# Attention inside a fused MLP kernel: phi's column maximum as one strided reduction on VectorE, and the scaling of the identity by it on GpSimd

## The chip, the core and the metric

One core of a Trainium2 chip runs the whole program. Its engines are TensorE (PE in the profile; its weight loads are PEld), VectorE (DVE), ScalarE (ACT), GpSimd (POOL) and SyncE (SP), which here only issues DMAs. Each engine takes its own instructions strictly in order and waits on semaphores for the others. The metric is the time of one execution on the device in microseconds, lower being better. The kernel before took 1745.2 us (median of 3 runs, 1739.94 to 1746.93).

## What is computed

```python
def _attn_ref(q, k, v, phi):                       # 8 batches, 8 heads, 576 rows, 64 wide; phi has 32 columns
    a = phi - np.max(phi, axis=2, keepdims=True)   # maximum over the 576 rows, per column
    a = np.exp(a)
    a = a / (np.sum(a, axis=2, keepdims=True) + 1e-09)
    k_m = np.einsum('bhsm,bhsd->bhmd', a, k)
    v_m = np.einsum('bhsm,bhsd->bhmd', a, v)
    scores = scale * np.matmul(q, k_m.transpose(0, 1, 3, 2))
    ...
    return np.matmul(attn, v_m)

# then, on the 4608 x 512 result:
h = x @ w_in;  x = (h - np.tanh(h)) @ w_out                              # layer 1, 2048 wide
h = x @ w_in;  out = np.where(h > 0, h, np.exp(np.minimum(h, 0)) - 1) @ w_out   # layer 2
```

The weights of the layers come as 64-bit floats and are converted on the chip.

## The kernel before

Attention is done in 16 units, each one batch and four of its heads. A unit's phi lies in SBUF as a tile `ph` of 96 partitions x 4 heads x 6 chunks x 32 columns: row s of phi is partition s // 6, chunk s % 6. Its column maximum is made in these steps (`Attention.unit`, lines 115 to 141):

- Lines 119 to 121, VectorE: the maximum over the six chunks in three elementwise operations: chunks 0 to 2 with 3 to 5 into `top` (384 elements per partition), then two of 128 elements into `cmax`. `top` takes a buffer of tag `pT`, of which there is one; the transposed weights `pT` of the unit before live in it until GpSimd's `phl` has read them.
- Line 127, TensorE: transposes `cmax` (96 x 128) into `mT`, a PSUM tile.
- Line 129, VectorE: `nmax`, the maximum of each row of `mT`: one number for each of the 128 pairs of head and column.
- Line 131, VectorE: `dmax`, the identity matrix with row i scaled by `nmax[i]`.
- Line 134, TensorE: `bmax` = ones x `dmax`, which spreads the 128 maxima over 96 partitions. Line 138, ScalarE: copies it to `bm`.
- Line 140: `a = ph - bm`, on VectorE in units 0 and 1, and on GpSimd from unit 2 on (`eng`). Line 146, ScalarE: exp.

After that TensorE contracts `a` with k and v into `km` (lines 155 and 158), VectorE divides by the sums (`rs`, `kk`, `vbd`, lines 164 to 170), and the scores (`sc`, `s`, `smax`, `pT`, `phl`) follow.

A unit is a Python generator. Each `yield` ends its part of a round, and one round of all live units is written out at a time, so the order of instructions on each engine is the order in which the program writes them; there is no scheduler behind it. From unit 2 on (`spaced`) some steps have an extra `yield`. The main loop goes over the blocks of layer 1 and has two rounds for each half of a block: one between the first and the second group of `x_ps` matmuls, one behind the second. In every half it writes: the matmuls `h_ps` of layer 1 (line 357), their activation on ScalarE (`t`, `u`, `s`, lines 368 to 370) and GpSimd (`v`, line 375), matmuls `x_ps` of the block four steps back (line 405), a round of the units and of the weights' conversion, the split of the previous activation `g` (ScalarE line 392, GpSimd line 393), more `x_ps`, then on VectorE the end of the activation (`h_ps`, `s`, `s`, lines 384 to 386), then again a round. The conversion of a piece of weights runs over ScalarE (`cv_m`, line 48), VectorE (`cv_m` and `cv_a`, lines 50 to 55), ScalarE (line 58) and GpSimd (`w`, line 60). `vw_ps` (lines 327 and 344) multiplies converted weights into the attention's value tiles. Units start at fixed rounds (0, 1, 7, 13, 23, 29, 35 and so on up to 99). PSUM tiles of the units, `x_ps` and `vw_ps` share three buffers. From about 440 us on attention is over; the rest of layer 1 and layer 2 (from about 900 us) follow.

Of the kernel before, what the change touches and what calls it, by code (L numbers as in the profile page):

```python
# [8 lines left out]
F32 = mybir.dt.float32  # L9
# [4 lines left out]
ALU = mybir.AluOpType  # L14
AX = mybir.AxisListType
# [3 lines left out]
B, H, S, D, M = 8, 8, 576, 64, 32  # L19
# [43 lines left out]
class Attention:  # L63
# [43 lines left out]
    def unit(self, u, nxt, eng, first_p=None):  # L107

        nc, wk, sm = self.nc, self.wk, self.sm
        b, g = divmod(u, 2)  # L110
        ident = self.ident
# [3 lines left out]
        ph = self.loaded.pop((u, "phi"))  # L115
        row = lambda name: wk.tile([128, 4, M], F32, tag="cmax", name=name)
        cmax = row("cmax")[:96]
        top = wk.tile([128, S], F32, tag="pT", name="top")[:96, :12 * M].rearrange("p (h c m) -> p h c m", h=4, c=3)
        nc.vector.tensor_tensor(top, ph[:, :, 0:3], ph[:, :, 3:6], op=ALU.max)
        nc.vector.tensor_tensor(cmax, top[:, :, 0], top[:, :, 1], op=ALU.max)  # L120
        nc.vector.tensor_tensor(cmax, cmax, top[:, :, 2], op=ALU.max)
        yield
        spaced = u >= 2
        if spaced:
            yield
        mT = ps_tile([128, 96], "mT")
        nc.tensor.transpose(mT, cmax.rearrange("p h m -> p (h m)"), ident[:96, :96])
        nmax = sm.tile([128, 1], F32, tag="nmax", name="nmax")
        nc.vector.tensor_reduce(nmax, mT, axis=AX.X, op=ALU.max)
        dmax = row("dmax").rearrange("p h m -> p (h m)")  # L130
        nc.vector.tensor_scalar(dmax, ident, nmax, None, op0=ALU.mult)
        yield
        bmax = ps_tile([96, 4, M], "bmax")
        nc.tensor.matmul(bmax, lhsT=self.ones[:, :96], rhs=dmax, start=True, stop=True)
        if spaced:
# [5 lines left out]
                          op=ALU.subtract)  # L141
# [74 lines left out]
        pT = wk.tile([128, S], F32, tag="pT", name="pT")  # L216
# [303 lines left out]
def moe_kernel(tc, q, k, v, phi, w1, w2, w3, w4, out):  # L520
    nc = tc.nc
    with ExitStack() as top, tc.manual_schedule():
# [105 lines left out]
        for u in range(2 * B):  # L628
            units.at((0, 1, 7, 13, 23, 29, 35, 41, 47, 53, 59, 65, 78, 85, 92, 99)[u], unit(u))
# [264 lines left out]
```

## Time and profile before

| | |
|---|---|
| median of 3 runs | 1745.2 us |
| the profiled execution | 1745.33 us, of it 1743.5 us span |
| TensorE busy | 1636.6 us (94%) |
| VectorE busy | 1220.5 us (70%) |
| ScalarE busy | 943.2 us (54%) |
| GpSimd busy | 766.4 us (44%) |
| TensorE's mean granted clock | 0.97 of full speed |

The profile is of one execution. Its timeline gives each instruction's start and duration, the idle time of its engine just before it, and what ended that idle time (an arrow to engine, tile and line). The waits sum such idle times by the waiting and the awaited instruction. The groups sum instructions of one line and shape. The table by stretches gives the busy time of each engine in a stretch of the span, so that the stages can be told apart. A busy TensorE is one that has matmuls under way; at half of its clock the same matmuls take up to twice as long.

### The profile page before, as it was taken

Reading aid. Unit: us, or ns where it says so; the run is one execution under the profiler, and the core shown is the slowest. Engines: PE = TensorE matmul, PEld = TensorE weight load, DVE = VectorE, ACT = ScalarE, POOL = GpSimd, SP = SyncE. Lnnn points to the kernel's source line nnn. Section 1 sums busy time; section 2 is a strip of 40 time slices with the busy share of each in tenths; the row PEclk is TensorE's granted clock in tenths of the full one; section 3 lists DMA queues with packets and bytes.
Section 4 is the critical chain, followed back from the end, with each engine's and each line's share of the span. In section 5 each row is a group of like instructions: output and inputs, shape, how many; then the busy total and the mean of one; then the engine's idle time right before and its main releaser. Section 6 shows DMA issues by size and latency. Waiting matters only on the chain.

```text
span 1743.5 us, 30389 instructions
## 1 busy us (share of the span) xinstructions
PE 1636.6 (94%) x11632; PEld 1513.9 (87%) x11632; DVE 1220.5 (70%) x1804; ACT 943.2 (54%) x1697; POOL 766.4 (44%) x545
## 2 busy tenths in 40 slices
PE   5659899898998999999989999999999999999998
PEld 4548888787898999999989999999999999999997
DVE  5778776678899999998965555555555555555554
ACT  2446756677878888898853333333333333333332
POOL 3246555545666676676752222222222222222222
PEclk9669999999998999999999999999999999999999
DMA  8755664567566456666588311211112112211110
GB/s 212 203 152 155 187 181 156 173 191 232 192 218 200 161 189 216 218 218 213 185 246 320 119 61 51 60 61 61 50 60 62 61 61 61 61 55 55 55 32 24
DMA packets 145000, 238.42 MB, mean 137 GB/s; under 512 B 12504, under 2 KB 106712, under 8 KB 142808
## 3 DMA queue, kind: packets, MB, share of 16 engines
q1 hardware_dynamic: 144856, 236.49, 42.7%
q8 instruction: 92, 1.51, 0.4%
q14 instruction: 52, 0.43, 0.1%
HBM read 159.78 MB, written 75.50 MB: 135 GB/s over the span
## 4 chain that ended last, share of the span: by engine, by line
PE 74%; DVE 9%; DMA 6%; ACT 6%; issue 3%; POOL 2%; SPq 0%; DVEq 0%; ACTq 0%; POOLq 0%
PE h_ps L461 24%; PE o_ps L498 23%; PE x_ps L405 15%; PE h_ps L357 8%; DMA p<-p_dram 2%; PE vw_ps L327 2%; DMA phi<-in_phi_dram 1%; ACT t L368 1%; PE vw_ps L344 1%; DVE s L386 1%; DVE s L385 1%; DMA kv<-in_v_dram 1%; DMA xr<-x_dram 1%; DMA w_dram<-wst 1%; ACT u L369 1%
## 5 line engine op out<-in xcount | busy, mean ns | idle before, releaser
L405 PE MATMUL x_ps<-g,w 128*128 128x288 f32 x3072 | 442.3, 298 | 9.1 <-DVE s L203 4.7
L487 POOL TENSOR_TENSOR e<-hm,e 128x512 fp32r<-128x512 f32 x144 | 186.5, 1295 | 587.1 <-ACT e L486 429.7
L461 PEld LDWEIGHTS h_ps<-x,wi 128*128 128x128 f32 x3456 | 429.7, 190 | 11.9 <-issue 0.2
L461 PE MATMUL h_ps<-x,wi 128*128 128x256 f32 x3456 | 433.3, 281 | 0.0
L405 PEld LDWEIGHTS x_ps<-g,w 128*128 128x128 f32 x3072 | 420.7, 190 | 13.5 <-DVE s L203 5.2
L498 PE MATMUL o_ps<-wo,e 128*128 128x512 f32 x1728 | 423.8, 394 | 0.7 <-POOL e L487 0.7
L498 PEld LDWEIGHTS o_ps<-wo,e 128*128 128x128 f32 x1728 | 314.8, 188 | 65.0 <-POOL e L487 1.1
L472 ACT ACTIVATE t_ps<-hm 128x512 f32<-128x512 f32 x144 | 86.7, 602 | 514.1 <-DVE hm L471 514.1
L375 POOL TENSOR_TENSOR v<-t,u 128x576 f32<-128x576 f32 x128 | 185.3, 1448 | 161.7 <-ACT u L369 151.1
L357 PE MATMUL h_ps<-p,vw 128*128 128x288 f32 x1536 | 237.8, 305 | 11.5 <-DVE s L386 5.9
L393 POOL TENSOR_TENSOR g<-s,g 128x576 fp32r<-128x576 f32 x128 | 198.7, 1552 | 97.9 <-ACT g L392 83.9
L478 DVE SCALAR_TENSOR_TENSOR hm<-hm,t_ps 128x512 f32<-128x512 f32 x144 | 99.0, 688 | 200.9 <-ACT hm L473 200.9
L357 PEld LDWEIGHTS h_ps<-p,vw 128*128 128x128 f32 x1536 | 217.8, 195 | 18.5 <-issue 14.4
L471 DVE TENSOR_SCALAR hm<-h_ps 128x512 f32<-128x512 f32 x144 | 99.6, 692 | 138.5 <-PE h_ps L461 138.5
L385 DVE SCALAR_TENSOR_TENSOR s<-s,v 128x576 f32<-128x576 f32 x128 | 133.0, 1039 | 1.5 <-POOL v L375 1.5
L368 ACT ACTIVATE t<-h_ps 128x576 f32<-128x576 f32 x128 | 83.2, 650 | 83.0 <-PE h_ps L357 33.6
L386 DVE COPY_PREDICATED s<-big,h_ps 128x576 f32<-128x576 uint32 x128 | 106.7, 834 | 11.5
L370 ACT ACTIVATE s<-u,bias 128x576 f32<-128x576 f32 x128 | 99.5, 778 | 23.1 <-POOL g L393 13.7
L480 DVE TENSOR_TENSOR hm<-hm,h_ps 128x512 f32<-128x512 f32 x144 | 99.0, 687 | 5.0
L479 DVE SCALAR_TENSOR_TENSOR hm<-hm,t_ps 128x512 f32<-128x512 f32 x144 | 99.0, 687 | 5.0
L384 DVE TENSOR_TENSOR h_ps<-h_ps,t 128x576 f32<-128x576 f32 x128 | 96.6, 754 | 2.6 <-ACT u L369 2.4
L473 ACT ACTIVATE hm<-hm 128x512 f32<-128x512 f32 x144 | 91.0, 632 | 13.7 <-ACT t_ps L472 0.7
(89 smaller groups left out, 1805.7 us busy)
## 6 DMA issues: line engine op xcount, KB each, us to landing
x_dram<-x SPq DMA_DIRECT2D x128, 288.0 KB
xr<-x_dram SPq DMA_DIRECT2D x72, 512.0 KB
p<-p_dram SPq DMA_DIRECT2D x62, 576.0 KB
raw<-in_moe_w_in_dram SPq DMA_DIRECT2D x32, 512.0 KB
raw<-in_moe_w_out_dram SPq DMA_DIRECT2D x32, 512.0 KB
w_dram<-wst SPq DMA_DIRECT2D x32, 512.0 KB
kv<-in_k_dram SPq DMA_DIRECT2D x16, 576.0 KB
kv<-in_v_dram SPq DMA_DIRECT2D x16, 576.0 KB
```

Source lines behind the costliest of these rows:

```text
L357: nc.tensor.matmul(ps[:, j, :NB], lhsT=vw[a][:, kc, 128 * j:128 * j + 128], rhs=p[:, kc, b, :], start=(k == 0), stop=(k == 5))
L368: nc.scalar.activation(t, w[0], ACTF.Tanh)
L370: nc.scalar.activation(s, u, ACTF.Square, bias=bias[:, 0:1], scale=G_S)
L375: nc.gpsimd.tensor_tensor(v, t, u, op=ALU.mult)
L385: nc.vector.scalar_tensor_tensor(s, s, G_B, v, op0=ALU.add, op1=ALU.mult)
L386: nc.vector.copy_predicated(s, big.bitcast(U32), d)
L393: nc.gpsimd.tensor_tensor(g[:, 1], s, r32(g[:, 0]), op=ALU.subtract)
L405: nc.tensor.matmul(ps, lhsT=wo[pg][:, a, j, 128 * dm:128 * dm + 128], rhs=g[:, b, j, :], start=(k == 0), stop=(k == 11))
L461: nc.tensor.matmul(ps[:, j], lhsT=w3[:, a, kc, 128 * j:128 * j + 128], rhs=x[:, b, kc, :], start=(k == 0), stop=(k == 11))
L471: nc.vector.tensor_scalar(hm, w[0], 0.0, None, op0=ALU.min)
L487: nc.gpsimd.tensor_tensor(e[:, 1], hm, r32(e[:, 0]), op=ALU.subtract)
L498: nc.tensor.matmul(self.acc[n][tg], lhsT=e[:, a, j, 128 * tg:128 * tg + 128], rhs=w4[:, b, j, :], start=(pg == 0 and j == 0 and i == 0), s ...
```

## The change

The column maximum becomes one VectorE reduction over the six chunks, read through a view in which the chunk is the innermost index; `top` and its buffer are not used any more. The extra `yield` of units 2 to 15 that stood ahead of the transposition `mT` now stands behind `nmax`, ahead of the scaling `dmax`; so `mT` and `nmax` come one round sooner, while `dmax` and all that follows keep their rounds. The scaling is issued on `eng`, which is VectorE in units 0 and 1 and GpSimd in units 2 to 15. Lines behind the change carry numbers three lower than before.

```diff
--- before.py
+++ after.py
@@ -115,20 +115,17 @@
         ph = self.loaded.pop((u, "phi"))
         row = lambda name: wk.tile([128, 4, M], F32, tag="cmax", name=name)
         cmax = row("cmax")[:96]
-        top = wk.tile([128, S], F32, tag="pT", name="top")[:96, :12 * M].rearrange("p (h c m) -> p h c m", h=4, c=3)
-        nc.vector.tensor_tensor(top, ph[:, :, 0:3], ph[:, :, 3:6], op=ALU.max)
-        nc.vector.tensor_tensor(cmax, top[:, :, 0], top[:, :, 1], op=ALU.max)
-        nc.vector.tensor_tensor(cmax, cmax, top[:, :, 2], op=ALU.max)
+        nc.vector.tensor_reduce(cmax, ph.rearrange("p h c m -> p h m c"), axis=AX.X, op=ALU.max)
         yield
         spaced = u >= 2
-        if spaced:
-            yield
         mT = ps_tile([128, 96], "mT")
         nc.tensor.transpose(mT, cmax.rearrange("p h m -> p (h m)"), ident[:96, :96])
         nmax = sm.tile([128, 1], F32, tag="nmax", name="nmax")
         nc.vector.tensor_reduce(nmax, mT, axis=AX.X, op=ALU.max)
         dmax = row("dmax").rearrange("p h m -> p (h m)")
-        nc.vector.tensor_scalar(dmax, ident, nmax, None, op0=ALU.mult)
+        if spaced:
+            yield
+        eng.tensor_scalar(dmax, ident, nmax, None, op0=ALU.mult)
         yield
         bmax = ps_tile([96, 4, M], "bmax")
         nc.tensor.matmul(bmax, lhsT=self.ones[:, :96], rhs=dmax, start=True, stop=True)
```

VectorE in unit 5, from the maximum to the row behind the scaling, before. `cv_m` and `cv_a` are steps of the weights' conversion, `smax`, `rs`, `kk` and `vbd` belong to the unit ahead:

```order
L119 TENSOR_TENSOR top<-phi 96x384
L120 TENSOR_TENSOR cmax<-top 96x128
L121 TENSOR_TENSOR cmax<-cmax,top 96x128
L54 SCALAR_TENSOR_TENSOR cv_m<-raw,cv_m 128x512
L55 SCALAR_TENSOR_TENSOR cv_a<-raw,cv_m 128x512
L50 TENSOR_SCALAR cv_m<-cv_m 128x512
```

```order
L164 TENSOR_SCALAR rs<-km 128x1
L165 RECIPROCAL rs<-rs 128x1
L167 TENSOR_SCALAR kk<-km,rs 128x128
L170 TENSOR_SCALAR vbd<-km,rs,pmask 128x64 x2
L129 TENSOR_REDUCE nmax<-mT 128x1
L131 TENSOR_SCALAR dmax<-ident,nmax 128x128
L54 SCALAR_TENSOR_TENSOR cv_m<-raw,cv_m 128x512
```

and after:

```order
L118 TENSOR_REDUCE cmax<-phi 96x128
L54 SCALAR_TENSOR_TENSOR cv_m<-raw,cv_m 128x512
L55 SCALAR_TENSOR_TENSOR cv_a<-raw,cv_m 128x512
L124 TENSOR_REDUCE nmax<-mT 128x1
L50 TENSOR_SCALAR cv_m<-cv_m 128x512
```

```order
L161 TENSOR_SCALAR rs<-km 128x1
L162 RECIPROCAL rs<-rs 128x1
L164 TENSOR_SCALAR kk<-km,rs 128x128
L167 TENSOR_SCALAR vbd<-km,rs,pmask 128x64 x2
L54 SCALAR_TENSOR_TENSOR cv_m<-raw,cv_m 128x512
```

Three rows have become one, `nmax` has gone up to stand before the conversion's next step, and `dmax` is gone from VectorE. In unit 3, VectorE before had, from the row behind the unit ahead's scaling of `s`:

```order
L213 RECIPROCAL smax<-smax 128x18
L214 TENSOR_TENSOR s<-s,smax 128x576
L54 SCALAR_TENSOR_TENSOR cv_m<-raw,cv_m 128x512
L55 SCALAR_TENSOR_TENSOR cv_a<-raw,cv_m 128x512
L217 STREAM_TRANSPOSE pT<-s 128x576
L211 TENSOR_REDUCE smax<-s 128x18
```

and after:

```order
L210 RECIPROCAL smax<-smax 128x18
L211 TENSOR_TENSOR s<-s,smax 128x576
L124 TENSOR_REDUCE nmax<-mT 128x1
L54 SCALAR_TENSOR_TENSOR cv_m<-raw,cv_m 128x512
L55 SCALAR_TENSOR_TENSOR cv_a<-raw,cv_m 128x512
L214 STREAM_TRANSPOSE pT<-s 128x576
L208 TENSOR_REDUCE smax<-s 128x18
```

There `nmax` now stands between `s` and the conversion. GpSimd in unit 5, before:

```order
L60 TENSOR_TENSOR w_955<-cv_a,w_955 128x512
L393 TENSOR_TENSOR g<-s,g 128x576
L214 TENSOR_TENSOR s<-s,smax 128x576
L60 TENSOR_TENSOR w_955<-cv_a,w_955 128x512
L222 TENSOR_TENSOR phl<-pT,phl 128x2x288
L140 TENSOR_TENSOR a<-phi,bm 96x4x6x32
```

and after:

```order
L60 TENSOR_TENSOR w_940<-cv_a,w_940 128x512
L390 TENSOR_TENSOR g<-s,g 128x576
L211 TENSOR_TENSOR s<-s,smax 128x576
L128 TENSOR_SCALAR dmax<-ident,nmax 128x128
L60 TENSOR_TENSOR w_940<-cv_a,w_940 128x512
L219 TENSOR_TENSOR phl<-pT,phl 128x2x288
L137 TENSOR_TENSOR a<-phi,bm 96x4x6x32
```

`dmax` stands there between `s` and the conversion's `w`, and in unit 4 likewise; in most of the later units it stands behind `g`. TensorE in unit 6, whose order units 7 to 11 repeat but for `vw_ps`, before:

```order
L155 MATMUL km<-kv,a 32x128 x24
L158 MATMUL km<-ones,a 128x2 x6
L405 MATMUL x_ps<-g,w_564 128x288 x6
L405 MATMUL x_ps<-g,w_748 128x288 x6
L180 MATMUL pq<-ident,q 128x96 x3
L127 MATMUL mT<-ident,cmax 128x96
L357 MATMUL h_ps<-p,vw 128x288 x12
L405 MATMUL x_ps<-g,w_564 128x288 x6
L405 MATMUL x_ps<-g,w_748 128x288 x6
L201 MATMUL sc<-qT,kT 64x288 x2
L180 MATMUL pq<-ident,q 128x96 x3
L134 MATMUL bmax<-dmax,ones 96x128
```

and after:

```order
L152 MATMUL km<-kv,a 32x128 x24
L155 MATMUL km<-ones,a 128x2 x6
L122 MATMUL mT<-ident,cmax 128x96
L402 MATMUL x_ps<-g,w_552 128x288 x6
L402 MATMUL x_ps<-g,w_736 128x288 x6
L177 MATMUL pq<-ident,q 128x96 x3
L354 MATMUL h_ps<-p,vw 128x288 x12
L402 MATMUL x_ps<-g,w_552 128x288 x6
L402 MATMUL x_ps<-g,w_736 128x288 x6
L198 MATMUL sc<-qT,kT 64x288 x2
L177 MATMUL pq<-ident,q 128x96 x3
L131 MATMUL bmax<-dmax,ones 96x128
```

`mT` has moved up from behind the next unit's `pq` to directly behind `km`; `bmax` has kept its place. ScalarE's and SyncE's orders are the same in both kernels.

## Rows read from the trace of the kernel before

**Rows 1.** Stretches: length, busy us (count) of PE, PEld, DVE, ACT, POOL; clock, DMA

```profile
20.00:62.00 42.00, 27.18 (x187) 20.52 (x179) 32.19 (x65) 15.26 (x37) 8.88 (x6) 0.80 0.72 196
62.00:108.00 46.00, 29.00 (x150) 21.33 (x151) 30.05 (x53) 20.31 (x40) 19.72 (x17) 0.61 0.63 183
108.00:152.00 44.00, 30.43 (x281) 27.61 (x281) 39.60 (x61) 25.44 (x51) 21.96 (x17) 0.83 0.59 164
152.00:300.00 148.00, 138.11 (x1251) 126.42 (x1251) 108.23 (x168) 95.75 (x195) 82.84 (x55) 1.00 0.57 174
300.00:440.00 140.00, 123.35 (x1046) 113.11 (x1044) 105.98 (x172) 98.12 (x193) 73.23 (x50) 0.99 0.62 191
```

**Rows 2.** Groups, VectorE, 20 to 440 us: xcount | busy us, mean ns | idle before

```profile
L119 DVE TENSOR_TENSOR top<-phi 96x384 f32<-96x384 f32 x14 | 14.4, 1030 | 6.2 <-POOL phl L222 5.1 <-DMA phi<-in_phi_dram 1.1
L120 DVE TENSOR_TENSOR cmax<-top 96x128 f32<-96x128 f32 x14 | 12.7, 904 | 0.6
L121 DVE TENSOR_TENSOR cmax<-cmax,top 96x128 f32<-96x128 f32 x14 | 12.0, 855 | 0.5
L131 DVE TENSOR_SCALAR dmax<-ident,nmax 128x128 f32<-128x128 f32 x14 | 11.2, 798 | 0.5
L206 DVE TENSOR_REDUCE smax<-s 128x18 f32<-128x576 f32 x14 | 10.3, 738 | 0.0
L211 DVE TENSOR_REDUCE smax<-s 128x18 f32<-128x576 f32 x14 | 10.3, 737 | 0.0
L129 DVE TENSOR_REDUCE nmax<-mT 128x1 f32<-128x96 f32 x14 | 3.4, 241 | 0.0
```

**Rows 3.** Timeline, unit 8: start us, us, engine, line, operation [idle before, releaser]

```profile
192.86 1.39 DVE L119 TENSOR_TENSOR top<-phi 96x384 f32<-96x384 f32 x1
...
194.49 1.50 PE L158 MATMUL km<-ones,a 128*128 128x2 f32 x12
...
201.46 1.41 POOL L375 TENSOR_TENSOR v<-t,u 128x576 f32<-128x576 f32 x1 [0.88 <-ACT u L369]
...
201.53 1.42 DVE L131 TENSOR_SCALAR dmax<-ident,nmax 128x128 f32<-128x128 f32 x1
```

**Rows 4.** TensorE's waits in 108:152, 152:300 and 300:440: us, times, longest

```profile
PE bmax L134 <- DVE dmax L131: 6.7, 2, 6.3
...
PE bmax L134 <- DVE dmax L131: 1.5, 4, 0.4
...
PE bmax L134 <- DVE dmax L131: 2.8, 1, 2.8
```

**Rows 5.** Timeline, unit 5

```profile
113.91 1.76 DVE L119 TENSOR_TENSOR top<-phi 96x384 f32<-96x384 f32 x1
...
118.50 0.39 PE L127 MATMUL mT<-ident,cmax 96*128 96x96 f32 x1 [3.17 <-DVE cmax L121]
...
123.11 1.16 POOL L214 TENSOR_TENSOR s<-s,smax 128x576 f32<-128x576 f32 x1 [4.91 <-DVE rs L164]
...
124.23 1.26 POOL L60 TENSOR_TENSOR w<-cv_a,w 128x512 fp32r<-128x512 f32 x1
...
125.72 0.71 PE L134 MATMUL bmax<-dmax,ones 128*96 128x128 f32 x2 [6.35 <-DVE dmax L131]
```

**Rows 6.** Timeline, unit 3

```profile
47.81 0.69 DVE L54 SCALAR_TENSOR_TENSOR cv_m<-raw,cv_m 128x512 uint32<-128x512 uint32 x1
...
49.30 0.40 PE L127 MATMUL mT<-ident,cmax 96*128 96x96 f32 x1
```

**Rows 7.** Timeline, unit 4

```profile
93.35 0.29 DVE L196 TENSOR_TENSOR vm<-kT_ps,vm 128x128 fp32r<-128x128 f32 x1 [0.93 <-ACT vm L195]
...
96.99 0.87 DVE L131 TENSOR_SCALAR dmax<-ident,nmax 128x128 f32<-128x128 f32 x1
```

**Rows 8.** Timeline, unit 12

```profile
325.28 0.56 DVE L119 TENSOR_TENSOR top<-phi 96x384 f32<-96x384 f32 x1 [3.38 <-POOL phl L222]
...
329.06 1.85 PE L405 MATMUL x_ps<-g,w 128*128 128x288 f32 x12 [2.16 <-DVE s L203]
```

**Rows 9.** Groups, GpSimd, 0 to 440 us

```profile
masks.py:199 POOL TENSOR_SCALAR_AFFINE_SELECT ident<-ident 128x128 f32<-128x128 f32 x1 | 0.3, 292 | 0.1
```

## Prediction

> **What bounds the kernel now.** I read the table by stretches first. Attention runs inside the first 440 us, laid over the first MLP layer. In its last two stretches, 152 to 440 us, TensorE is busy for 261 of 288 us at full clock; from 20 to 152 us it is busy for 87 of 132 us at a mean clock of 0.6 to 0.8, and VectorE is the fuller engine in each of those three stretches, with 39.60 of 44 us in the tightest one [rows 1]. So the early part waits for VectorE and for latency, and the later part has little idle TensorE time to give: 14.8, 17.0, 13.6, 9.9 and 16.7 us in the five stretches (stretch less PE busy). All that the change touches lies before 440 us; afterwards the instructions are the same, so what is won or lost by then is handed on to the end.
>
> Next the groups of VectorE's instructions. In units 2 to 15 the three maxima take 14.4 + 12.7 + 12.0 = 39.1 us and the scaling of the identity 11.2 us [rows 2]. Means of 855 ns and more for 128 elements are odd, and the timeline of unit 8 tells why: the scaling starts at 201.53 and takes 1.42 us, ending 0.08 us after GpSimd's v, which began just before it [rows 3]. An operation on VectorE that reads SBUF this way stands until GpSimd's instruction is through. The existing reductions don't do this: 28 of them over 576 elements take 0.737 and 0.738 us on average, whatever GpSimd does [rows 2].
>
> Last, TensorE's waits. It stands 6.7, 1.5 and 2.8 us in three stretches at bmax for the scaled identity [rows 4], and in unit 5 it stands 3.17 us at mT for the maximum and 6.35 us at bmax [rows 5].
>
> **The maximum.** One reduction over 768 elements replaces 640 elements in three instructions. The nearest row is the reduction of 576 at 0.738 us [rows 2]; at its rate 768 cost 0.98 us, which I take. It reads phi at a step of 128 bytes (32 fp32), which no row of VectorE does. The lower end is the same 0.98 us. The upper end is the slowest row of top, 1.76 us for 384 elements [rows 5], which gives 3.5 us. At 0.98 us the 14 units cost 13.7 us, so VectorE is relieved of 39.1 + 11.2 - 13.7 = 36.6 us in all. The scratch tile top also goes. It shared its buffer with pT, so in unit 12 it waited 3.38 us for GpSimd's phl [rows 8].
>
> The Trainium skill speaks against this, in "Advanced Engine Details and Errata", SBUF Cachelines: where each access falls in another 16-byte line, there is a performance penalty. It gives no price. By it the forecast is the rival C below; no row here shows such a read.
>
> **The scaling on GpSimd.** 14 instructions over 128 columns. GpSimd's only other instruction on that shape takes 0.29 us [rows 9], its s over 576 elements takes 1.16 us [rows 5]; I take 0.4 us, near the first, since the shape decides most of it. That is 14 x 0.4 = 5.6 us on an engine that is busy for 83 of 148 us [rows 1]. It stands in GpSimd's queue after g in most units, where GpSimd then waits for ScalarE anyway; in units 4 and 5 it stands between s and the conversion's w, which I count there. Elsewhere I charge 0.5 us in all.
>
> **The order.** mT comes a round earlier on TensorE, directly behind km from unit 6 to 11, and nmax a round earlier on VectorE; the scaling keeps its round and bmax too. So VectorE now waits for TensorE at nmax with the conversions and the three operations that end a block's activation (h_ps, s, s) behind it, and TensorE waits at mT with x_ps or vw_ps behind it. In unit 8 the maximum starts at 192.86 and km ends at 194.49 + 1.50 = 195.99 [rows 3], so there is a slack of 3.1 us for a reduction of 0.98 us. It holds there; I take the same for units 7 and 9 to 11, which have the same order.
>
> **Unit by unit, on the path.**
> - Unit 3: VectorE reached the conversion at 47.81, where nmax now stands first, and mT ends at 49.30 + 0.40 = 49.70 [rows 6]. It would stand 1.9 us in a stretch where VectorE sets the pace. Cheaper work of units 2 and 3 gives back about half: +1.0 us.
> - Unit 4: what is saved before 93.35 is lost, since VectorE stands there for ScalarE (0.93 us). Behind that point the scaling of 0.87 us and nmax of 0.24 us no longer lie ahead of the conversion [rows 2, 7]: -1.1 us.
> - Unit 5: the maximum starts at 113.91 and ends just before mT at 118.50 [rows 5], 4.4 us; now 0.98, so 3.5 us sooner. GpSimd's s, behind it in the chain, goes from 123.11 to 119.6, plus 0.24 for nmax ahead of it, ends at 121.0, the scaling at 121.4. bmax stood at 125.72. What is late next is the conversion's w on GpSimd, 1.26 us [rows 5], which the fifth matmul of vw_ps needs: 122.7 us, where vw_ps began behind bmax at 126.4 (125.72 + 0.71) and its fifth matmul ran a little later. I take -4.0 us, not the 9.5 us that TensorE stood.
> - Units 6 to 11: bmax's other waits go, 0.4 + 1.5 us [rows 4, 5]: -1.9 us. TensorE's small waits at mT for a free accumulator move with mT and stay.
> - Unit 12: VectorE no longer stands 3.38 us, and x_ps, which waited 2.16 us for VectorE's transposition behind it, starts on time [rows 8]: -2.2 us. mT, closer to its maximum now, may take some of it.
> - Unit 15: bmax's 2.8 us [rows 4] go; GpSimd gets the scaling behind g, well before. -2.5 us.
> - The rest of the relief is off the path until it reaches TensorE through g. Of 9.9 + 16.7 us of idle TensorE time in the last two stretches, 1.5 + 2.2 + 2.8 are used above; of the 20 left I take a seventh, because most are waits for ScalarE: -3 us.
>
> Sum: 1.0 - 1.1 - 4.0 - 1.9 - 2.2 - 2.5 + 0.5 - 3.0 = -13.2 us. The profiled execution took 1745.33 us, with a span of 1743.5, and the median of the runs is 1745.2, so both serve alike: 1745.3 - 13.2 = 1732 us. TensorE's clock is the part that no row fixes: it stood at half speed for parts of 20 to 152 us [rows 1], and a denser stretch can raise it or a shifted one lower it. I leave 4 us either way.
>
> **The rivals.**
> A is the forecast: 1732, with 1724 to 1740 as its own range.
> B, VectorE's whole relief arrives. If VectorE sets the pace in all five stretches, 36.6 us go, less what 152 to 300 us can't take: five units bring 5 x 36.6 / 14 = 13.1 us there against 9.9 us of idle TensorE time. 36.6 - 3.2 = 33 us: 1712 us. For it speaks that VectorE is 90% busy at 108 to 152 us; against it that TensorE is busy for 93% of the stretch behind that.
> C, the strided reduction costs twice as much, 1.97 us. The 14 x 0.98 us extra fall mostly into slack (1.97 is below 3.1). On the path are units 2 and 3 with 2 us, unit 5 with 1, unit 12 with 1, and half of the general 3 us: 13.2 - 5.5 = 7.7 us, so 1737.6. The Trainium skill's rule on cachelines, named above, would make it so. The change also does little if GpSimd's scaling takes 1.16 us: 0.76 us more in units 4, 5 and at four places from 300 us on is 4.6 us, 1737.
> D, slower: the reduction takes longer than the slack. From 3.1 us on TensorE stands at mT, with x_ps and h_ps queued behind it, while VectorE is loaded beyond what it saved. At 5 us (6.5 ns an element) TensorE would stand 1.9 us in 11 units, 5 to 15, which is 21 us, while the waits at bmax that go are worth 0.4 + 1.5 + 2.8 and unit 5's 4: 1745 + 21 - 9 = 1757. Against it: the upper end from rows is 3.5 us, at which the loss at mT is 0.4 us a unit and the time about 1741.
>
> **How the numbers follow.** A 0.50, B 0.17, C 0.23, D 0.10. The likeliest is A, 1732. The range reaches down to nearly B and up past C to the time before: 1714 to 1745. Over 0.5% (8.7 us, about what a measurement of this kernel can tell from no change) means below 1736.5: most of A (0.43), B, and a part of C (0.06), 0.66. Slower by as much, above 1753.9, is D, 0.09. Within it is the rest, 0.25.
>
> **What would show it.** Right: the reduction near 0.98 us in every unit, alike beside GpSimd's work; the scaling on GpSimd at 0.3 to 0.5 us; TensorE's waits at bmax nearly gone; unit 3's nmax standing about 2 us for mT; the shift grown to some 4 us by 152 us and to 13 by 440, and constant after that. Wrong: a reduction over 1.5 us; TensorE standing at mT or at pq for nmax in the middle units; a shift that grows or shrinks behind 440 us; another share of half clock before 152 us.

## The result and the profile after

The changed kernel takes 1728.55 us (median of 5 runs, 1727.47 to 1733.39) against 1746.01 us for the kernel before in the same rounds (5 runs, 1739.94 to 1746.98): a ratio of 0.9906, 95% interval 0.9889 to 0.9924. It is faster by about 16 us, 3.5 us below the forecast of 1732 and inside its range.

The span of the profiled execution is 1726.6 us, 16.9 us less than before. The table by stretches, after (columns as in [rows 1]):

```profile
20.00:62.00 42.00, 27.15 (x167) 19.12 (x159) 32.43 (x58) 15.23 (x37) 10.03 (x8) 0.88 0.70 192
62.00:108.00 46.00, 28.16 (x152) 21.71 (x153) 28.61 (x51) 20.68 (x40) 20.39 (x18) 0.63 0.66 187
108.00:152.00 44.00, 34.73 (x323) 31.89 (x322) 36.32 (x61) 27.28 (x54) 24.08 (x20) 0.92 0.64 175
152.00:300.00 148.00, 140.19 (x1276) 128.99 (x1275) 97.24 (x160) 99.60 (x204) 82.80 (x62) 1.00 0.59 178
300.00:440.00 140.00, 126.30 (x1077) 115.99 (x1076) 107.43 (x165) 103.82 (x207) 83.91 (x59) 1.00 0.64 200
```

From 108 to 152 us TensorE is busy for 4.3 us more than in [rows 1], at a clock of 0.92 instead of 0.83, and VectorE, which was busy for 39.60 of 44 us there, is busy for 3.3 us less (the changed kernel is some 5 us ahead by 150 us, so the stretches do not hold quite the same work); from 152 us on TensorE has 7.8 and 13.7 us of idle time left where it had 9.9 and 16.7.

The groups of VectorE's and GpSimd's instructions, 20 to 440 us (columns as in [rows 2], which holds what they replace):

```profile
L118 DVE TENSOR_REDUCE cmax<-phi 96x128 f32<-96x768 f32 x14 | 21.2, 1514 | 2.8 <-DMA phi<-in_phi_dram 2.8
L124 DVE TENSOR_REDUCE nmax<-mT 128x1 f32<-128x96 f32 x14 | 3.5, 250 | 6.9 <-PE mT L122 6.8
L128 POOL TENSOR_SCALAR dmax<-ident,nmax 128x128 f32<-128x128 f32 x14 | 9.5, 678 | 25.6 <-DVE nmax L124 25.6
```

The reduction takes 1.51 us, not 0.98, and the scaling 0.68 us, not 0.4. So VectorE loses 39.1 + 11.2 and gets 21.2: a relief of 29.1 us, where 36.6 were forecast. New is that VectorE stands 6.8 us at `nmax` for TensorE's transposition: a round earlier and behind a short maximum, VectorE is there before TensorE. In the runs below that keep the order of before or the three maxima, it stands under 1 us there.

TensorE's waits, after (us in total, times, longest), first the lines that answer to [rows 4], those of 108 to 152 us, then those of 152 to 300 and of 300 to 440 us:

```profile
PE bmax L131 <- POOL dmax L128: 5.9, 1, 5.9
...
PE km L152 <- ACT x L409: 4.2, 4, 1.1
PE sc L198 <- ACT kT L189: 3.1, 4, 0.8
PE mT L122 <- DVE cmax L118: 0.2, 1, 0.2
...
PE x_ps L402 <- DVE s L200: 2.4, 2, 1.5
...
PE bmax L131 <- POOL dmax L128: 0.2, 1, 0.2
```

In the last two stretches the waits at `bmax` for the scaling are gone (0.2 us of 4.3), and `x_ps` waits 2.4 us for VectorE's `s`, where it waited 4.7 us in the trace of before:

```profile
PE x_ps L405 <- DVE s L203: 4.7, 3, 2.2
```

From 108 to 152 us, one wait of 5.9 us stands where one of 6.3 stood, and unit 5's rows show why it is worth so much less. Timeline of unit 5, after (to lay beside [rows 5]):

```profile
113.36 1.52 DVE L118 TENSOR_REDUCE cmax<-phi 96x128 f32<-96x768 f32 x1
...
115.02 0.28 PE L122 MATMUL mT<-ident,cmax 96*128 96x96 f32 x1 [0.54 <-DVE cmax L118]
...
119.64 1.16 POOL L211 TENSOR_TENSOR s<-s,smax 128x576 f32<-128x576 f32 x1 [2.33 <-DVE rs L161]
120.77 0.60 POOL L128 TENSOR_SCALAR dmax<-ident,nmax 128x128 f32<-128x128 f32 x1
121.34 1.28 POOL L60 TENSOR_TENSOR w<-cv_a,w 128x512 fp32r<-128x512 f32 x1
...
121.43 0.74 PE L131 MATMUL bmax<-dmax,ones 128*96 128x128 f32 x2 [5.89 <-POOL dmax L128]
```

TensorE still stands long at `bmax`, but reaches it sooner: `bmax` starts at 121.43, which is 4.3 us ahead of the 125.72 of before. The scaling ends at 121.37 and the conversion's `w` at 122.62, where 121.4 and 122.7 were forecast.

How the shift grows, read from the start of ScalarE's `bm` in each unit, before and after:

| unit | before | after | shift |
|---|---|---|---|
| 3 | 60.15 | 60.21 | +0.1 |
| 4 | 101.24 | 100.69 | -0.6 |
| 5 | 131.47 | 127.22 | -4.3 |
| 6 | 158.18 | 152.56 | -5.6 |
| 8 | 205.88 | 198.77 | -7.1 |
| 11 | 282.69 | 273.51 | -9.2 |
| 12 | 336.33 | 325.55 | -10.8 |
| 14 | 389.93 | 378.39 | -11.5 |
| 15 | 419.46 | 405.39 | -14.1 |

Between ScalarE's instructions of layer 1 the shift is -4.7 us at 150, -13.5 at 447, -13.9 at 793 and -16.9 at the end. The last 3 us come between 793 and 920 us, where both kernels run the same instructions; the experiments below return to that. In what follows "the shift at 447" is this same reading: the start of one and the same ScalarE instruction, which before ran at 447 us, less its start before.

### The profile page after: what moved, and what is told of

It reads as the page before. It is cut to its first block, busy times and chain, and to the rows that moved or that the text cites. A ratio compares the mean times of both kernels' runs of the same rounds, so it can differ in the third digit from the quotient of the medians.

```text
span 1726.6 us, 30354 instructions
## 1 busy us (share of the span) xinstructions
PE 1632.3 (95%) x11632; PEld 1511.1 (88%) x11632; DVE 1192.7 (69%) x1758; ACT 942.5 (55%) x1697; POOL 771.8 (45%) x559
## 3 DMA queue, kind: packets, MB, share of 16 engines
q8 instruction: 92, 1.51, 0.4%
## 4 chain that ended last, share of the span: by engine, by line
PE 79%; ACT 7%; DVE 4%; issue 3%; DMA 3%; POOL 2%; SPq 0%; ACTq 0%; DVEq 0%; POOLq 0%
PE h_ps L458 24%; PE o_ps L495 23%; PE x_ps L402 17%; PE h_ps L354 10%; PE vw_ps L324 2%; DMA phi<-in_phi_dram 1%; ACT t L365 1%; PE km L152 1%; PE vw_ps L341 1%; PE km L155 1%; ACT u L366 1%; POOL g L390 1%; ACT big L376 1%; ACT s L367 1%; DMA raw<-in_moe_w_in_dram 1%
## 5 line engine op out<-in xcount | busy, mean ns | idle before, releaser
L402 PEld LDWEIGHTS x_ps<-g,w 128*128 128x128 f32 x3072 | 419.5, 189 | 10.8 <-issue 3.0
L354 PEld LDWEIGHTS h_ps<-p,vw 128*128 128x128 f32 x1536 | 218.2, 195 | 15.6 <-issue 11.1
L470 ACT ACTIVATE hm<-hm 128x512 f32<-128x512 f32 x144 | 91.0, 632 | 13.7 <-ACT t_ps L469 0.8
```

What stands on the lines that cost most here:

```text
L354: nc.tensor.matmul(ps[:, j, :NB], lhsT=vw[a][:, kc, 128 * j:128 * j + 128], rhs=p[:, kc, b, :], start=(k == 0), stop=(k == 5))
L402: nc.tensor.matmul(ps, lhsT=wo[pg][:, a, j, 128 * dm:128 * dm + 128], rhs=g[:, b, j, :], start=(k == 0), stop=(k == 11))
```

## The experiments

All ratios are to the kernel before, from the same rounds. The change has three parts: the reduction, the order (the `yield` behind `nmax` instead of ahead of `mT`) and the place of the scaling. The first six experiments are the other combinations of the three.

**The reduction alone.**

```diff
-        top = wk.tile(...)
-        nc.vector.tensor_tensor(top, ph[:, :, 0:3], ph[:, :, 3:6], op=ALU.max)
-        ...
+        nc.vector.tensor_reduce(cmax, ph.rearrange("p h c m -> p h m c"), axis=AX.X, op=ALU.max)
```

> The kernel before with the strided reduction alone; mT, nmax and the scaling stay where they were, on VectorE. In the changed kernel the reduction takes 1.51 us (mean of 14), not 0.98. Theory T (the gain is VectorE time that stood behind GpSimd's instructions): VectorE is relieved of 39.1 - 21.2 = 18 us, unit 5's maximum ends 2.9 us sooner and with it bmax, unit 12 no longer waits 3.4 us for the buffer of pT; 6 to 8 us in all, 1738 to 1740. Rival R (the gain is the scaling's distance to bmax and its other engine): at most 3 us, 1743 to 1746.

1736.47 us (1735.01 to 1738.68), ratio 0.9946 [0.9928, 0.9965]: some 9.4 us of the gain, a little more than T gave it and far from R. The reduction takes 1526 ns here, and the shift at 447 is -8.0. TensorE still waits for the scaling on VectorE; the lines for it, of 20 to 108, 108 to 152 and 300 to 440 us, are

```profile
PE bmax L131 <- DVE dmax L128: 11.8, 3, 6.1
...
PE bmax L131 <- DVE dmax L128: 7.1, 2, 6.7
...
PE bmax L131 <- DVE dmax L128: 2.8, 1, 2.8
```

At these places the waits at `bmax` are as long as before or longer, only the 1.5 us of 152 to 300 us are gone, and more than half of the gain is there. 2.5 us of the shift come in unit 12 (-5.3 to -7.7), where `top` had waited for the buffer of `pT`. The three maxima with a buffer of their own for `top` were not run, so how much of the reduction's worth is the buffer is not separated.

**Order and GpSimd, with the three maxima kept.**

```diff
-        nc.vector.tensor_reduce(cmax, ph.rearrange("p h c m -> p h m c"), axis=AX.X, op=ALU.max)
+        top = wk.tile(...)
+        nc.vector.tensor_tensor(top, ph[:, :, 0:3], ph[:, :, 3:6], op=ALU.max)
+        ...
```

(this diff and the following ones are against the changed kernel, where nothing else is said)

> The changed kernel with the three maxima of before: mT and nmax a round earlier, the scaling on GpSimd. T: VectorE loses only the scaling's 11.2 us; TensorE's waits at bmax in units 6 to 15 go (0.4 + 1.5 + 2.8 us), but in unit 5 mT still waits for the maximum that ends at 118.4, and in units 8 and 10 mT now stands behind a maximum that ends 1 us after km; 4 to 6 us, 1740 to 1742. R: 13 to 17 us, 1729 to 1733.

1750.97 us (1746.08 to 1756.24), ratio 1.0024 [1.0009, 1.0039]: not faster at all, but a little slower than before. Both expectations missed. The shift at 447 is +6.9. TensorE's waits for the maximum, of 20 to 108, 108 to 152, 152 to 300 and 300 to 440 us:

```profile
PE mT L125 <- DVE cmax L121: 4.6, 2, 3.5
...
PE mT L125 <- DVE cmax L121: 2.7, 2, 1.9
...
PE mT L125 <- DVE cmax L121: 6.2, 5, 1.5
...
PE mT L125 <- DVE cmax L121: 4.2, 1, 4.2
```

That is 17.7 us, against 1.4 + 2.6 + 0.5 + 0.2 = 4.7 us in the changed kernel. The order puts `mT` a round closer to the maximum. Three operations aren't through by then, in the middle units neither (in units 7 to 10 they run for 4.2 to 4.3 us and end about 1 us behind `km`), so `x_ps` and `h_ps` stand behind `mT`. What is rival D of the prediction does happen, only not with the reduction. The 4.2 us from 300 us on have another cause: they are unit 12, where the three take 1.2 us but `top` starts 3.3 us late, for the buffer that GpSimd's `phl` still reads.

**Order alone.** As the run before, and the scaling back on VectorE:

```diff
-        eng.tensor_scalar(dmax, ident, nmax, None, op0=ALU.mult)
+        nc.vector.tensor_scalar(dmax, ident, nmax, None, op0=ALU.mult)
```

> The three maxima of before, mT and nmax a round earlier as in the changed kernel, the scaling still on VectorE in its old round. T: nothing is taken off VectorE, and in units 8 to 11 TensorE stands about 1 us at mT for the maximum: 1745 to 1750. R, in so far as the order is what gains: 1735 to 1740.

1751.41 us (1748.90 to 1756.14), ratio 1.0032 [1.0021, 1.0044]; the waits at `mT` for the maximum are 4.2, 3.9, 5.9 and 4.2 us in the four stretches, the shift at 447 is +8.4. So it is the order that costs, and in this order the place of the scaling hardly counts (0.4 us in the medians, 1.5 in the shift). The median is 1.4 us above what T gave.

**The scaling alone.** Against the kernel before:

```diff
-        nc.vector.tensor_scalar(dmax, ident, nmax, None, op0=ALU.mult)
+        eng.tensor_scalar(dmax, ident, nmax, None, op0=ALU.mult)
```

> The kernel before with the scaling of units 2 to 15 on GpSimd, in the place where it stood; the three maxima and the order stay. Theory P: taking the scaling off VectorE is worth its 4 us whatever stands beside it (with the reduction it took 1736.5 to 1732.4): 1740 to 1743 us, and bmax no longer waits in 152 to 300 us. Rival Q: without the short maximum the scaling's input is as late as before, VectorE is as loaded with the maxima, and the move only trades VectorE's wait for GpSimd's queue (w, g and s ahead of it): 1744 to 1748 us, with TensorE's waits at bmax before 152 us as long as before, now for GpSimd.

1739.61 us (1736.07 to 1743.97), ratio 0.9958 [0.9944, 0.9972]: P, and a little more. The waits at `bmax` in 152 to 300 us are gone, as P said; before 152 us they stay as long (10.4 + 5.8 us, for GpSimd now), as Q said. The shift at 447 is -3.8, the price that P named, and 2.7 us more come behind 793 us, where nothing was changed. That it is worth this whatever stands beside it does not hold: in the new order with the three maxima the same move gave 1.5 us in the shift (the two runs above).

**Reduction and order, without GpSimd.**

```diff
-        eng.tensor_scalar(dmax, ident, nmax, None, op0=ALU.mult)
+        nc.vector.tensor_scalar(dmax, ident, nmax, None, op0=ALU.mult)
```

> The changed kernel with the scaling back on VectorE, in the round it has in both kernels: the reduction and the earlier mT and nmax. If the earlier order is what pays once the reduction is short: 1728 to 1731. If GpSimd is what pays: near the reduction alone (1736.5), 1735 to 1739, with the waits at bmax in 300 to 440 us (2.8) back.

1734.84 us (1732.91 to 1739.35), ratio 0.9935 [0.9920, 0.9951], shift at 447 of -9.5: 1.5 us better in the shift than the reduction alone, with intervals that overlap, and about what was expected if GpSimd is what pays. The waits at `bmax` for VectorE are still there, 10.1, 5.8 and 1.8 us.

**Reduction and GpSimd, without the order.**

```diff
+        if spaced:
+            yield
         mT = ps_tile([128, 96], "mT")
...
-        if spaced:
-            yield
         eng.tensor_scalar(dmax, ident, nmax, None, op0=ALU.mult)
```

> The reduction, and the scaling on GpSimd, in the order of before (mT, nmax and the scaling in one round, a round ahead of bmax). If GpSimd is what pays: 1729 to 1732. If the earlier nmax is needed for it, because GpSimd now gets its scaling only behind VectorE's late nmax: 1735 to 1740, with TensorE's waits at bmax as long as with the reduction alone (7.1 us in 108 to 152, 2.8 in 300 to 440).

1732.39 us (1731.36 to 1737.49), ratio 0.9923 [0.9908, 0.9938], shift at 447 of -12.7: nearly all of the shift of the changed kernel, just past the upper end of what was expected if GpSimd is what pays. TensorE's waits for the scaling are as long as ever before 152 us (11.1 + 6.1 us) and 1.4 us from 300 us on.

All eight together, with the shift at 447 us; the times hold in addition the scatter of what follows:

| maximum | order | scaling | time, us | ratio | shift at 447 |
|---|---|---|---|---|---|
| three | old | VectorE | 1746.0 | 1 | 0 |
| three | new | VectorE | 1751.4 | 1.0032 [1.0021, 1.0044] | +8.4 |
| three | old | GpSimd | 1739.6 | 0.9958 [0.9944, 0.9972] | -3.8 |
| three | new | GpSimd | 1751.0 | 1.0024 [1.0009, 1.0039] | +6.9 |
| one | old | VectorE | 1736.5 | 0.9946 [0.9928, 0.9965] | -8.0 |
| one | new | VectorE | 1734.8 | 0.9935 [0.9920, 0.9951] | -9.5 |
| one | old | GpSimd | 1732.4 | 0.9923 [0.9908, 0.9938] | -12.7 |
| one | new | GpSimd | 1728.6 | 0.9906 [0.9889, 0.9924] | -13.5 |

The reduction is worth 8 to 9 us in the old order and 18 to 20 in the new one; the scaling on GpSimd about 4 in three of its four pairs; the order costs 8 to 11 us with three maxima and gives 0.8 to 1.5 with one (all by the shift). The last is less than what the times can tell: the intervals overlap in both pairs.

**Does the stride matter?** The same reduction, reading phi as it lies in memory:

```diff
-        nc.vector.tensor_reduce(cmax, ph.rearrange("p h c m -> p h m c"), axis=AX.X, op=ALU.max)
+        nc.vector.tensor_reduce(cmax, ph.rearrange("p h c m -> p (h c m)").rearrange("p (h m c) -> p h m c", h=4, c=6), axis=AX.X, op=ALU.max)
```

> The changed kernel, with the reduction reading the same 768 elements of phi in their order in memory; so the maxima are taken over the wrong groups, and the output is not the reference's. If the step of 128 bytes is what the reduction pays for, it takes 0.94 to 0.98 us here instead of 1.51, VectorE has 7.5 us less in units 2 to 15, and the time is 1 to 3 us below the changed kernel's, 1726 to 1728. If 1.51 us is what 128 separate results cost (576 elements to 18 results took 0.74), the duration stays 1.4 to 1.5 us and so does the time.

1729.86 us (1729.23 to 1734.74), ratio 0.9912 [0.9894, 0.9929], no different from the changed kernel. Its groups, 20 to 440 us:

```profile
L118 DVE TENSOR_REDUCE cmax<-phi 96x128 f32<-96x768 f32 x14 | 13.0, 926 | 3.0 <-DMA phi<-in_phi_dram 2.9
L124 DVE TENSOR_REDUCE nmax<-mT 128x1 f32<-128x96 f32 x14 | 3.5, 250 | 11.4 <-PE mT L122 11.4
```

The step of 128 bytes costs 1514 - 926 = 588 ns an operation, 8.2 us of VectorE in 14 units. So the duration came much as expected, but the 1 to 3 us of time did not come: at 150 us this kernel is 2.8 us ahead of the changed one, and by 447 us little of that is left. In the place of the 8.2 us VectorE stands 4.5 us longer at `nmax` for `mT`, and the shift at 447 is -14.4, within 1 us of the changed kernel's. What the Trainium skill ("Advanced Engine Details and Errata", SBUF Cachelines) says without a price, that accesses which each fall in another 16-byte line are slower, the trace agrees with: 1.51 against 0.93 us. As a price on the path (rival C) it came to nothing.

**Where does more VectorE work begin to cost?** The reduction issued twice:

```diff
         nc.vector.tensor_reduce(cmax, ph.rearrange("p h c m -> p h m c"), axis=AX.X, op=ALU.max)
+        nc.vector.tensor_reduce(cmax, ph.rearrange("p h c m -> p h m c"), axis=AX.X, op=ALU.max)
```

> The changed kernel with the reduction issued twice, so that the maximum takes 3.0 us in every unit: 42 us of VectorE in units 2 to 15, more than the three maxima cost in the run with the order and GpSimd (36.9 us, 2.6 a unit, but 4.2 in the crowded units). Theory S (what counts is whether the maximum ends inside the 3.1 us between its start and the end of km): TensorE's waits at mT in 152 to 300 us stay under 1.5 us (6.2 there with the three maxima), and the time is 1731 to 1737. Rival L (VectorE's total load counts): 1745 to 1752, as with the three maxima.

1741.90 us (1737.48 to 1746.03), ratio 0.9969 [0.9956, 0.9982], between S and L. 21.0 us more of VectorE cost 13 us in the medians and 9.4 in the shift at 447 (-4.1). Of these, 5.0 us are lost by 150 us (shift +0.3). TensorE's waits at `mT` are 7.3, 2.1, 1.0 and 2.6 us in the four stretches: in the middle one they stay at 1.0 for 3.0 us of reduction, as S said and as the prediction's slack of 3.1 us wants it. So a longer maximum does not cost through `mT` there. That 3.0 us fit where the three maxima, 2.6 us a unit on average, did not, is a matter of the single unit: in units 7 to 10 the three took 4.2 to 4.3 us and the two reductions take 3.1. The second reduction costs most in the early part, where VectorE is fullest; there the waits at `mT` are 9.4 us against 4.5 in the changed kernel, and the 4.9 us more are about what is lost by 150 us, but whether these waits or VectorE's load cost it was not told apart. Between 150 and 307 us another 2.8 us are lost, for which no wait at `mT` stands, and 1.6 behind that.

**Are the waits at bmax in units 4 and 5 on the path?** The scaling a round sooner, with `nmax`, on GpSimd:

```diff
         nc.vector.tensor_reduce(nmax, mT, axis=AX.X, op=ALU.max)
         dmax = row("dmax").rearrange("p h m -> p (h m)")
+        eng.tensor_scalar(dmax, ident, nmax, None, op0=ALU.mult)
         if spaced:
             yield
-        eng.tensor_scalar(dmax, ident, nmax, None, op0=ALU.mult)
```

> The changed kernel with the scaling on GpSimd in the round of nmax instead of the one behind it. In the changed kernel TensorE still stands 3.4 and 5.9 us at bmax in units 4 and 5, because the scaling stands behind GpSimd's s, which waits for VectorE. If these waits are on the path, they go and the time falls by 2 to 4 us, 1724.5 to 1726.5. If what follows bmax there is late for another reason (the conversion's w), the waits go and the time stays, 1727 to 1730.

1729.72 us (1729.28 to 1730.23), ratio 0.9900 [0.9884, 0.9916]: the changed kernel's time. TensorE's waits of 108 to 152 us:

```profile
PE vw_ps L341 <- POOL w L60: 3.0, 1, 3.0
PE mT L122 <- DVE cmax L118: 1.8, 1, 1.8
PE bmax L131 <- POOL dmax L126: 1.7, 1, 1.7
```

4.2 of the 5.9 us at `bmax` are gone, and 3.0 us at `vw_ps` for GpSimd's `w` and 1.3 more at `mT` have come in their place. So `bmax` was mostly the first place at which TensorE met what was late there. The prediction's choice of -4.0 us, not 9.5, for unit 5 rested on this. Quite nothing the waits are not: from unit 3's `bm` to 150 us this kernel gains 6.3 us and the changed one 4.8, for the 7.5 us by which the waits at `bmax` are shorter before 152 us. At unit 3 it was 1.7 us behind the changed kernel, with a granted clock of 0.57 instead of 0.88 from 20 to 62 us, which hides the difference at 150 us; at 447 us the two kernels are level (-13.6 and -13.5).

**Is GpSimd needed, or is it enough that VectorE loses the scaling?**

```diff
-        eng.tensor_scalar(dmax, ident, nmax, None, op0=ALU.mult)
+        if spaced:
+            nc.scalar.activation(dmax, ident, ACTF.Copy, scale=nmax)
+        else:
+            nc.vector.tensor_scalar(dmax, ident, nmax, None, op0=ALU.mult)
```

> The changed kernel with the scaling of units 2 to 15 on ScalarE in place of GpSimd (a copy with a scale per partition). Theory M: what the move pays for is that the scaling leaves VectorE, where it stood behind other work or beside GpSimd's (the reduction and the order alone gave 1734.8 us with it on VectorE); the engine that takes it is nearly free to choose. Then the time is 1727 to 1732 us, ScalarE's scaling takes 0.3 to 0.5 us in each unit, and bmax waits for it less than the 5.9 and 3.4 us that it waits for GpSimd's in units 5 and 4. Rival N: ScalarE stands for nmax at the scaling, with the activation of layer 1 (t, u, s) and the conversion's steps queued behind it, and GpSimd was the one engine with room at that place. Then 1733 to 1740 us, and ScalarE's idle time ahead of the scaling is above 5 us before 440 us.

1733.11 us (1729.92 to 1736.34), ratio 0.9942 [0.9926, 0.9957]: by the median at the lower end of N's range, and the interval does not touch the changed kernel's. The six runs lie at 1729.9 to 1730.9 and at 1735.4 to 1736.3 us, three each, and the profile is of one of the lower three. Its rows speak for M. ScalarE's group, 20 to 440 us:

```profile
L129 ACT ACTIVATE dmax<-ident,nmax 128x128 f32<-128x128 f32 x14 | 5.6, 397 | 0.0
```

ScalarE never stands ahead of it, where N wanted over 5 us; `bmax` waits 2.3 us in unit 5 instead of 5.9 (and `vw_ps` 3.2 us for GpSimd's `w`, as with the sooner scaling); the shift is -13.2 at 447, as with GpSimd (-13.5). The two part behind that: -14.6 against -13.9 at 793, and -14.4 against -16.8 at 921. In that last stretch the experiments scatter without any tie to what they change: -2.9 (the changed kernel), -2.2, -2.7 and -2.3 us (reduction alone, scaling alone, reduction twice) up to +2.3 (reduction and GpSimd). No instruction there is changed, and TensorE stands at `h_ps` once for 4 to 6 us there, before layer 2. So up to 447 us ScalarE serves as well as GpSimd. In time GpSimd is the better one on these runs, by 4.6 us in the medians; what parts the two behind 447 us stays open. And about 3 of the 16.9 us by which the changed kernel's profiled execution is shorter come from a stretch in which no step of the change lies. None of the runs is clearly faster than the changed kernel; the sooner scaling and the dense reduction are level with it.

## Why the prediction came out right, step by step

**What bounds the kernel.** Right: the gain was made in the attention's part, and the shift grew up to 447 us and then held until 793. The 3 us behind that were not foreseen, and a shift that grows behind 440 us is one of the prediction's own signs of being wrong. The unchanged stretch before layer 2 scatters by as much from kernel to kernel, so they may be no part of the change; that stays open. Without them the profiled execution gained 13.9 us, against the sum's 13.2, and the interval of the ratio, 13 to 19 us, takes in both readings. A second such sign came too, another clock before 152 us: 0.88, 0.63 and 0.92 of full speed in the three stretches, where it had been 0.80, 0.61 and 0.83. What that gave is not told apart from the rest; the prediction had left 4 us for it.

**The reduction** is the term that was mis-sized: 1.51 us (1.45 to 1.58 in units 2 to 15) against 0.98, and inside the range of 0.98 to 3.5. The cause is the stride, 0.59 us, which the dense reduction took away. It is alike beside GpSimd's work, as forecast. In unit 4 it started 0.04 us behind GpSimd's v and was through in 1.51 us:

```profile
89.66 1.41 POOL L372 TENSOR_TENSOR v<-t,u 128x576 f32<-128x576 f32 x1 [2.36 <-ACT u L366]
89.70 1.51 DVE L118 TENSOR_REDUCE cmax<-phi 96x128 f32<-96x768 f32 x1
91.33 0.18 PEld L122 LDWEIGHTS mT<-ident,cmax 96*128 96x128 f32 x1 [2.80 <-issue]
91.36 0.39 PE L122 MATMUL mT<-ident,cmax 96*128 96x96 f32 x1 [2.59 <-DVE cmax L118]
```

VectorE's scaling, which began in the same way just behind v, stood until v was through [rows 3]. So did the three maxima. The second and the third in unit 8, before:

```profile
193.80 1.72 POOL L375 TENSOR_TENSOR v<-t,u 128x576 f32<-128x576 f32 x1
194.29 1.38 DVE L120 TENSOR_TENSOR cmax<-top 96x128 f32<-96x128 f32 x1
195.48 1.46 POOL L393 TENSOR_TENSOR g<-s,g 128x576 fp32r<-128x576 f32 x1
195.70 1.39 DVE L121 TENSOR_TENSOR cmax<-cmax,top 96x128 f32<-96x128 f32 x1
```

Each ends 0.15 us behind the GpSimd instruction beside it. In units 7 to 10 the three so take 4.2 to 4.3 us; in units 2, 12 and 13, where GpSimd does nothing beside them, 1.20 us in all, less than the reduction. The reduction is not the quicker work, it is the work that does not stand for GpSimd. The Trainium skill ("SBUF — State Buffer", Who interferes with whom) says that a reduction never contends with GpSimd on this chip, and the trace agrees in units 2 to 15. (The one long reduction, 1.98 us in unit 1, overlaps a scaling on VectorE, issued just ahead of it; both end at the same moment, 0.08 us behind a memset of GpSimd.) By the prediction's own test (a reduction over 1.5 us is a wrong sign) it was in C's direction, a half of the way to C's 1.97 us. But C's price was too high: the dense reduction gave nothing back.

**The scaling on GpSimd**: 0.68 us on average, 0.59 to 1.11 (the longest in units 14 and 15), above the 0.3 to 0.5 expected; the nearest row by shape was a poor guide. The 0.28 us more in 14 units meet 25.6 us that GpSimd stands ahead of it for `nmax`.

**Unit 3**: the stall of 1.9 us did not come. Timeline, to lay beside [rows 6]:

```profile
47.84 0.28 PE L122 MATMUL mT<-ident,cmax 96*128 96x96 f32 x1
48.16 0.26 DVE L124 TENSOR_REDUCE nmax<-mT 128x1 f32<-128x96 f32 x1 [0.47 <-PE mT L122]
48.33 0.69 DVE L54 SCALAR_TENSOR_TENSOR cv_m<-raw,cv_m 128x512 uint32<-128x512 uint32 x1
```

VectorE stands 0.47 us. The step had left `mT` where it ended before, at 49.70; but the transposition moved as well and ended at 48.12. The step had taken the place of VectorE's instruction from the order after and that of TensorE's from the trace before. By the end of the unit the shift is +0.1 (from -0.4 in unit 2), where +1.0 was forecast.

**Units 4 and 5**: -0.6 and -3.7 us against -1.1 and -4.0. The chain in unit 5 ran as written, to 0.2 us; the reduction that was 0.5 us longer had begun 0.55 us sooner, so that the closeness of the hit is in part luck. By 150 us the shift is -4.7, where -4.1 was forecast. TensorE's waits at `bmax` there did not nearly vanish, as the list of signs had it (0.9 + 3.4 + 5.9 us before 152 us): its first part is wrong for the early units, and the experiment with the sooner scaling shows that this wait is only a small loss.

**Units 6 to 11**: -4.9 us against -1.9 and a share of the -3 for the rest. Two waits are gone by name, 1.5 us at `bmax` and the 1.3 us at `mT` for a free accumulator, where 0.2 us for the maximum are new. The second one was forecast to move with `mT` and to stay; directly behind `km` it finds its accumulator free. It stayed, 1.3 us, in all three runs with the old order (reduction alone, reduction and GpSimd, scaling alone). Between 150 and 307 us the shift grows by 2.4 us with the reduction alone, by 1.8 with the order added, by 2.4 with GpSimd added, and by 4.5 with both (by 2.2 with the dense reduction, which was 2.8 us further ahead at 150 us). Some 2 us of it no wait names. Unit 8's slack held as forecast: the reduction started at 186.70 and `km` ended at 189.82, 3.1 us later, and twice the reduction still fitted in.

```profile
186.70 1.54 DVE L118 TENSOR_REDUCE cmax<-phi 96x128 f32<-96x768 f32 x1
...
188.32 1.50 PE L155 MATMUL km<-ones,a 128*128 128x2 f32 x12
...
190.00 0.26 DVE L124 TENSOR_REDUCE nmax<-mT 128x1 f32<-128x96 f32 x1 [1.09 <-PE mT L122]
```

**Units 12 to 15**: -1.6 and -2.5 us against -2.2 and -2.5, with -0.8 between them. The wait for `phl` is gone with `top`, and so is `bmax`'s wait of 2.8 us. The rest of the relief, -3 us, is spread over units 6 to 14; from 150 to 447 us the whole is -8.8, and the terms for it add up to -9.1. So the sum was right in the total, with unit 3 too dear and units 6 to 11 too small by 3.0 us. The general -3 us made up for the latter: a seventh of the idle time, which no row fixed, so that its size came out is luck. The reduction's 0.53 us too little cost at most 0.9 us at 447 us, by the dense reduction's shift.

**The rivals.** B, all of the relief, is out: of 29.1 us, 13.5 had arrived by 447 us. Nor has a microsecond of VectorE one price: 8.2 us less (the dense reduction) gave nothing, and 21.0 us more (the reduction twice) cost 9.4 to 13 us. D is out for the reduction as it came, but its mechanism is real, and it was much nearer than its 0.10 and its price of 5 us a reduction had it: with three maxima the new order is some 5 us slower than before. Its limit, the slack of 3.1 us, held: two reductions of 3.1 us fit in the middle units, three maxima of 4.2 did not. What the prediction did not say is that the parts are not a sum. The order does no harm only because the maximum is short.

## What to carry to other kernels

A step that is moved closer to its producer is priced together with the producer's duration: here the same move of one `yield` cost some 5 us behind three operations and gave 1.6 and 3.8 us in the medians behind one (0.8 and 1.5 in the shift, hardly clear of the scatter), so the parts of such a change are to be tried together. Before a wait on the busiest engine is counted as a gain, look at what it would wait for next; of two waits of 3.4 and 5.9 us most could be taken away for next to no gain, since other waits came up in their place. An operation is priced beside what runs at its side: the one reduction takes longer than the three maxima do when alone, and about a third of their time in the crowded units. When a row of the old trace and a row of the new order meet in one estimate, both ends of the wait have to be moved.

## What the chip showed besides

- A strided operation may take 1.6 times as long as the same one dense and still be the better choice: 768 elements at a step of 128 bytes took 1.51 us, dense 0.93, and the three operations on 640 elements 1.03 + 0.90 + 0.86 = 2.79 us on average [rows 2], against 1.20 us where GpSimd did nothing beside them; the rest is time in which VectorE stood for GpSimd.
- The scaling of 128 x 128 by a number per partition took 0.40 us on ScalarE, 0.68 on GpSimd and 0.80 on VectorE [rows 2]. On VectorE with the three maxima, but in the new order, it took 0.52 us: the place decides as much as the engine. In units 14 and 15 GpSimd needed 1.11 us for it.
- TensorE's granted clock from 20 to 62 us was 0.53 to 0.92 of full speed in these kernels, between the levels of 1.2 and 2.4 GHz. At unit 3's `bm`, some 60 us in, the kernels with 0.53 to 0.60 stood at +0.3 to +3.1 us and those with 0.80 to 0.92 at -1.2 to +1.4. By 150 us no tie is left: 0.57 with the sooner scaling and 0.88 in the changed kernel, which stand at -4.6 and -4.7 us there. From 20 to 62 us TensorE is idle for a third of the time and more, so that what it wins by its clock it can lose again by waiting; that this is the reason was not tested.
